# One order for all engines from the first pass on, in an attention and two feed-forward layers

## The chip, the cores and the metric

The kernel runs on one core of one Trainium2 chip. The metric is device time in microseconds (us) of one execution. Engines are called as the profile calls them: PE is TensorE's matmul queue and PEld its weight loads, DVE is VectorE, ACT is ScalarE, POOL is GpSimd, SP is SyncE, which issues the DMAs.

## What is computed

12480 tokens of 128 numbers go through an attention over 32 learned rows and then through two feed-forward layers of width 2048:

```python
h   = mab(I, x)                    # the 32 rows attend to all tokens
x1  = mab(x, h)                    # all tokens attend to the 32 results
a   = x1 @ w_in;  g = a * clip(a + 3, 0, 6) / 6
x2  = g @ w_out                    # first layer, 128 -> 2048 -> 128
r   = max(x2 @ w2_in, 0);  out = (r * r) @ w2_out   # second layer
# mab(q, kv): softmax(q @ kv.T / sqrt(128)) @ kv
```

The weights arrive as 64-bit floats.

## The kernel before

**Tiles and stages.** A first part, up to about 37 us, forms `h` from all tokens. Then the tokens run in 25 chunks of 512 (the last two 384 and 320), each in eight steps, so that a step `k` is a chunk `k // 8` and a pair of 128-wide slices `k % 8` of the 2048. The steps are numbered through, 0 to 199. A loop (L740) holds for each step `k`: `up1(k)` on PE (L575, two matmuls into a PSUM tile `h`), `gate1(k)` (ACT L588, then DVE L589), `high1` and `low1`, which split the gated tile into a rounded upper part and the rest, and `down1(k-2)`, which adds the step's share to `yacc`. The second layer follows eleven steps behind with `up2`, `relu2`, `square2`, `high2`, `low2` and `down2(k-14)`. At the end of a chunk `yacc` becomes `yh` (ACT L645) and `yl` (DVE L646).

**Two forms of a down matmul.** With both operands split, `down` (L621) issues six short matmuls in the fp32r form (L628). For the first steps, `k < N1` in the first layer and `k < N2` in the second, `down_whole` (L612) takes the unsplit tile and the unsplit weights in two fp32 matmuls (L616, each two records in the trace). A step in that form has no `high` and no `low`. N1 is 12 and N2 is 4.

**Weights.** Each of the four matrices comes in four pieces `a0` to `d3` (a: first up, b: first down, c: second up, d: second down). A conversion has a first stage (DVE L180 and L184, ACT L189), a second (DVE L191 and L195) and a third, an addition on POOL (L200). A cut then makes an upper part on ACT (L211) and a lower on DVE (L214). The `a` pieces are multiplied with the attention's result, `mix` (PE L455), `mix_high` (ACT L461) and `mix_low` (DVE L465), into the four quarters of `m4`, which `up1` reads.

**PSUM.** One pool of three buffers (`hp`, tag `h`) holds in turn the attention's scores `ps`, the products `mixed`, the turned weights `pt` and the tiles of `up1` and `up2`.

**What sets the order.** Up to `first.close()` (L733), and from step `KM` = 24 on, each engine runs its instructions in the order in which the program writes them. Between, a scheduler chooses the order of PE, DVE, ACT and POOL; only SP keeps the written order throughout. `PLAN` gives each weight piece the tick at which its conversion and its cut are handed to the scheduler, two ticks a step. From step 24 on, POOL first runs a one-column copy `turn` (L791) that reads the last tile DVE wrote in the step, and then `high1(k)`, so that POOL starts when DVE has come to that place.

Of the kernel before, what the change touches and what calls it, by code (L numbers as in the profile page):

```python
# [38 lines left out]

PLAN = {  # L40
    ("a", 0): (4, None),
    ("a", 1): (6, None),
    ("a", 2): (8, None),
    ("a", 3): (9, None),
    ("b", 0): (11, 51),
    ("b", 1): (16, 55),
    ("b", 2): (19, 42),
    ("b", 3): (23, 47),
    ("c", 0): (30, 33),
    ("c", 1): (35, 38),  # L50
    ("c", 2): (44, 47),
    ("c", 3): (50, 53),
    ("d", 0): (41, 59),
    ("d", 1): (47, 63),
    ("d", 2): (52, 55),
    ("d", 3): (55, 58),
}

CUTS = {"b": (2, 3, 0, 1), "c": (0, 1, 2, 3), "d": (2, 3, 0, 1)}

HIGH1_S = {13, 14, 18, 19, 20, 22, 23}
HIGH2_P = {6, 7, 10, 12}
N1, N2 = 12, 4
OFF = 11
L1, L2 = 2, 3
MIX = (0, 2, 4)
PRE = 22
KM = 24
# [7 lines left out]
def induced_attention_then_two_ffn(  # L76
# [93 lines left out]
    def lower_of(item):  # L170
        kind, q = item
        n = CUTS[kind].index(q)
        tag = f"w{kind}{CUTS[kind][n - 1]}" if n else {"b": "lb", "c": "lc", "d": "wc3"}[kind]
        return (wpool if kind == "b" else wpool2).tile([P, CW], F32R, tag=tag, name="wl")

    def convert(item):
        words = raws.pop(item)
# [12 lines left out]
        yield  # L190
        nc.vector.tensor_scalar(  # L191
            out=e, in0=e, scalar1=3, scalar2=0x3FFFFFFF,
            op0=ALU.logical_shift_left, op1=ALU.bitwise_and,
        )
        nc.vector.scalar_tensor_tensor(  # L195
            out=e, in0=high, scalar=0xC0000000, in1=e, op0=ALU.bitwise_and, op1=ALU.bitwise_or,
        )
        yield
# [7 lines left out]
    def cut(item):  # L206
        kind, q = item
        hi = (wpool if kind == "b" else wpool2).tile([P, CW], F32R, tag=f"h{kind}{q}", name="wh")
        w = whole.pop(item)
        assert ("a", q) not in whole or kind != "b"  # L210
        nc.scalar.copy(hi, w)  # L211
        yield
        lo = lower_of(item)
        nc.vector.tensor_tensor(out=lo, in0=w, in1=hi, op=ALU.subtract)  # L214
        parts[item] = hi, lo

# [5 lines left out]
    live, ticks = [], []  # L222

    def tick():
        n = len(ticks)
        ticks.append(n)
        for g in list(live):
            if next(g, live) is live:
                live.remove(g)
        for item, (when, cut_at) in PLAN.items():  # L230
            if when == n:
                load_until(item)
                live.append(convert(item))
                next(live[-1])
        for item, (when, cut_at) in PLAN.items():
            if cut_at == n:
                live.append(cut(item))
                next(live[-1])
# [16 lines left out]
    first = ExitStack()  # L255
    first.enter_context(tc.manual_schedule())
# [264 lines left out]
    def att_norm(c):  # L521
        a = att_weights(c)
        att[c] = a
        if c < TURNS:
# [3 lines left out]
            for u in range(2):  # L528
                last = nc.vector.tensor_tensor(
# [3 lines left out]
            return last  # L533
# [3 lines left out]
    def att_turn(c):  # L537
        a4 = att.pop(c)
        pt = hp.tile([P, CH], F32, tag="h", name="pt")
        to = pt.rearrange("p (b k t) -> p k b t", b=J, k=J)  # L540
# [6 lines left out]
        return nc.scalar.copy(a_t[c], pt)  # L547
# [45 lines left out]
    def high1(k):  # L593
# [3 lines left out]
        if k in HIGH1_S:  # L597
# [76 lines left out]
    def high2(k):  # L674
# [3 lines left out]
        if k in HIGH2_P or K - TAIL <= k < K - 1:  # L678
# [55 lines left out]
    behind = ExitStack()  # L734
    behind.enter_context(tc.issue_after(on_vector.ins))
    behind.enter_context(tc.issue_after(on_scalar.ins))
    for n in range(3):
        tick()
    assert len(ticks) == PRE, len(ticks)
    for k in range(K + OFF + L2 + 1):  # L740
        if k == KM:
            behind.close()
            ctx.enter_context(tc.manual_schedule())
# [3 lines left out]
        if k < KM:  # L747
            on(low1, k - 1)
        tick()
        on(gate1, k)  # L750
        if k < KM:
            on(high1, k)
# [13 lines left out]
        if k >= KM:  # L766
            on(down1, k - L1)
            on(down2, j - L2)
        behind_it = lo1[k - 1][:, 0, :1].bitcast(F32) if KM <= k < K else None
        if c + 1 < NCH:  # L770
            if p == 0 and LAST < c + 2 < NCH:
                load_x(c + 2)
            if p == 0:
                att_scores(c + 1)
                behind_it = att_shift(c + 1)
            if p == 1:
                att_exp(c + 1)
            if p == 2:
                behind_it = att_norm(c + 1)
            if p == 3:  # L780
                if c + 1 < TURNS:
                    att_turn(c + 1)
                else:
                    behind_it = att_spread(c + 1)
        if k < KM:
            on(down1, k - L1)
            on(down2, j - L2)
        elif k < K:

            n = behind_it.shape[0]  # L790
            nc.gpsimd.tensor_copy(turn[:n], behind_it)  # L791
            high1(k)
# [28 lines left out]
```

## Time and profile before

| | us |
|---|---|
| median of three runs (979.56 to 981.21) | 979.84 |
| profiled execution, its own time | 980.15 |
| its span in the trace | 978.4 |
| PE busy | 958.4 |
| DVE busy | 813.0 |
| ACT busy | 819.8 |
| POOL busy | 249.4 |

Busy time of PE counts modelled ends of matmuls that overlap, so the distance between starts of the same matmul in successive steps says more. A wait in brackets behind a row is the idle time of that engine just ahead of the instruction and what ended it. PEclk is the granted clock of TensorE as a share of full speed; its two levels are 2.4 GHz (1.00) and 1.2 GHz (0.50).

### The profile page before, as it was taken

What the parts mean: (1) busy time and instruction counts of PE and PEld (TensorE: products, weight loads), DVE (VectorE), ACT (ScalarE), POOL (GpSimd) and SP (SyncE); (2) the same over time, 40 slices, a digit from 0 to 9 for tenths busy, and PEclk for the clock granted to TensorE, in tenths of its full rate; (3) what the DMA queues carried; (4) which work ended last, traced back from release to release, by engine and by line L of the source; (5) the groups of instructions that cost most, each with busy time, mean ns of one, the idle gap of its engine ahead of it and who ended that gap; (6) DMA issues with size and microseconds to landing.
All of it is one profiled execution on the core that took longest, in us unless ns stands there. A gap on an engine that the chain in (4) does not pass through costs nothing.

```text
span 978.4 us, 12902 instructions
## 1 busy us (share of the span) xinstructions
PE 958.4 (98%) x4601; PEld 768.9 (79%) x4601; DVE 813.0 (83%) x999; ACT 819.8 (84%) x932; POOL 249.4 (25%) x390
## 2 busy tenths in 40 slices
PE   9789899999999999999999999999999999999998
PEld 7445588888888888888888888888888888888898
DVE  5889979888888888888888888888888888888774
ACT  6657798888888888888888888888888888888887
POOL 1222412222222222222222222222222222222222
PEclk9789999999999999999999999999999999999999
DMA  9610010010010110110110110110110100100000
GB/s 358 238 56 21 1 34 6 27 33 6 27 33 6 28 33 5 30 33 3 30 33 3 30 33 3 31 33 1 32 33 1 33 25 7 29 19 1 18 12 15
DMA packets 32111, 34.28 MB, mean 35 GB/s; under 512 B 7600, under 2 KB 24368, under 8 KB 31536
## 3 DMA queue, kind: packets, MB, share of 16 engines
q1 hardware_dynamic: 32048, 33.47, 11.0%
q8 instruction: 36, 0.59, 0.2%
q14 instruction: 27, 0.22, 0.1%
HBM read 21.18 MB, written 6.39 MB: 28 GB/s over the span
## 4 chain that ended last, share of the span: by engine, by line
PE 91%; DVE 5%; ACT 1%; POOL 1%; issue 1%; POOLq 0%; DVEq 0%
PE oacc L628 27%; PE h L657 26%; PE yacc L628 25%; PE h L580 9%; DVE g L589 1%; PE ps L478 1%; PE yacc L616 1%; POOL w L200 1%; PE xt L332 1%; DVE wl L214 1%; DVE lo L608 1%; PE s L312 1%; DVE cve L195 0%; DVE cve L184 0%; PE hacc L357 0%
## 5 line engine op out<-in xcount | busy, mean ns | idle before, releaser
L589 DVE SCALAR_TENSOR_TENSOR g<-g,h 128x1024 f32<-128x1024 f32 (+2 forms) x200 | 238.7, 1193 | 118.8 <-ACT g L588 115.2
L588 ACT ACTIVATE g<-h,three 128x1024 f32<-128x1024 f32 (+2 forms) x200 | 218.8, 1094 | 117.4 <-PE h L580 114.5
L692 DVE TENSOR_TENSOR lo<-g,hi 128x1024 fp32r<-128x1024 f32 (+3 forms) x197 | 235.0, 1193 | 9.7 <-PE oacc L628 6.0
L608 DVE TENSOR_TENSOR lo<-g,hi 128x1024 fp32r<-128x1024 f32 (+2 forms) x188 | 224.6, 1195 | 3.0 <-POOL hi L600 3.0
L672 ACT ACTIVATE g<-g 128x1024 f32<-128x1024 f32 (+3 forms) x201 | 206.0, 1025 | 0.4
L668 ACT ACTIVATE g<-h 128x1024 f32<-128x1024 f32 (+3 forms) x201 | 198.6, 989 | 4.8 <-PE h L657 3.6
L600 POOL TENSOR_SCALAR hi<-g 128x1024 fp32r<-128x1024 f32 (+2 forms) x181 | 187.4, 1035 | 22.9 <-DVE g L589 22.6
L684 ACT CAST hi<-g 128x1024 fp32r<-128x1024 f32 (+1 forms) x186 | 191.5, 1030 | 0.0
L657 PE MATMUL h<-yh,wh 128*128 128x512 f32 (+2 forms) x400 | 154.9, 387 | 3.8 <-DVE g L589 3.4
L657 PE MATMUL h<-yl,wh 128*128 128x512 f32 (+2 forms) x400 | 155.3, 388 | 0.0
L657 PE MATMUL h<-yh,wl 128*128 128x512 f32 (+2 forms) x400 | 154.9, 387 | 0.0
L580 PE MATMUL h<-at,m 128*128 128x512 f32 (+2 forms) x400 | 133.2, 414 | 3.6 <-ACT at L547 2.6
L628 PE MATMUL oacc<-hi,wh 128*128 128x512 f32 (+2 forms) x392 | 118.9, 384 | 0.0
L628 PE MATMUL oacc<-hi,wl 128*128 128x512 f32 (+2 forms) x392 | 118.9, 384 | 0.0
L628 PE MATMUL oacc<-lo,wh 128*128 128x512 f32 (+2 forms) x392 | 118.9, 384 | 0.0
L628 PE MATMUL yacc<-hi,wh 128*128 128x512 f32 (+2 forms) x376 | 114.4, 385 | 1.6 <-DVE yl L646 1.6
L628 PE MATMUL yacc<-hi,wl 128*128 128x512 f32 (+2 forms) x376 | 114.3, 385 | 0.0
L628 PE MATMUL yacc<-lo,wh 128*128 128x512 f32 (+2 forms) x376 | 113.7, 384 | 0.0
L791 POOL COPY turn<-lo 128x1 f32<-128x1 f32 x113 | 21.4, 189 | 343.4 <-DVE lo L608 343.4
L580 PEld LDWEIGHTS h<-at,m 128*128 128x128 f32 x400 | 74.3, 191 | 30.0 <-issue 9.5
L657 PEld LDWEIGHTS h<-yh,wh 128*128 128x128 f32 x400 | 75.1, 188 | 21.4 <-DVE g L589 4.2
L657 PEld LDWEIGHTS h<-yl,wh 128*128 128x128 f32 x400 | 75.2, 188 | 15.6 <-issue 0.2
(112 smaller groups left out, 926.0 us busy)
## 6 DMA issues: line engine op xcount, KB each, us to landing
outT<-osb SPq DMA_DIRECT2D x23, 256.0 KB, 2.2
xc<-in_xT SPq DMA_DIRECT2D x21, 256.0 KB, 2.8
xg<-in_xT SPq DMA_DIRECT2D x4, 1024.0 KB, 6.9
at<-ah SPq DMA_DIRECT2D x168, 16.0 KB, 1.8
at<-al SPq DMA_DIRECT2D x168, 16.0 KB, 1.8
raw<-in_w1a SPq DMA_DIRECT2D x4, 512.0 KB, 8.7
raw<-in_w1b SPq DMA_DIRECT2D x4, 512.0 KB, 7.5
raw<-in_w2a SPq DMA_DIRECT2D x4, 512.0 KB, 9.2
```

The costliest lines, as they stand in the source:

```text
L580: nc.tensor.matmul(h1[k][:, u, :size[c]], lhsT=m4[:, f * P:(f + 1) * P], rhs=a_t[c], start=True, stop=True)
L588: nc.scalar.activation(g1[k], h, AF.Relu, bias=three)
L589: nc.vector.scalar_tensor_tensor(out=g1[k], in0=g1[k], scalar=6.0, in1=h, op0=ALU.min, op1=ALU.mult)
L600: nc.gpsimd.tensor_scalar(out=hi1[k], in0=g1[k], scalar1=1.0, scalar2=1.0, op0=ALU.mult, op1=ALU.mult)
L608: nc.vector.tensor_tensor(out=lo1[k], in0=g1.pop(k), in1=hi1[k], op=ALU.subtract)
L628: nc.tensor.matmul(acc, lhsT=w[:, f * P:(f + 1) * P], rhs=g[:, u, :], start=(p == 0 and n == 0), stop=(p == NP - 1 and n == 5),)
L657: nc.tensor.matmul(h2[k][:, u, :size[c]], lhsT=w, rhs=y, start=(n == 0), stop=(n == 2))
L668: nc.scalar.activation(g2[k][:, u, :], h[:, u, :n], AF.Relu)
L672: nc.scalar.activation(g2[k][:, u, :], g2[k][:, u, :], AF.Square)
L684: nc.scalar.copy(hi2[k][:, u, :], g2[k][:, u, :])
L692: nc.vector.tensor_tensor(out=lo2[k][:, u, :], in0=g[:, u, :], in1=hi2[k][:, u, :], op=ALU.subtract)
L791: nc.gpsimd.tensor_copy(turn[:n], behind_it)
```

## The change

The order is now written out for all engines from the first pass to the end (`ctx.enter_context(tc.manual_schedule())` ahead of the first part). `PLAN`, `CUTS` and the two sets that chose an engine for the upper parts go. Tables say in which tick (`EARLY`) or step (`LATER`, `BESIDE`) a conversion's stages `1`, `2`, `3`, and the cuts `h` (upper) and `l` (lower), stand. What is named in `BESIDE` runs on POOL behind the one-column copy `turn`, now from before step 0: all third stages from `b1` on, and four of the lower parts (`b0`, `b1`, `c0`, `c1`). The other lower parts stay on DVE. `N1` goes from 12 to 16 and `N2` from 4 to 8. Of the `mix` products, two are now ahead of step 0 and the others in steps 2 and 3. The first chunk's scores are computed with the tokens in the partitions, so that its DVE transpose goes, and eight transposes of the identity (`fill`) stand on PE ahead of the first `pt`.

```diff
-    ("b", 0): (11, 51),
...
-    ("d", 3): (55, 58),
+LATER = {
+    0: "b3.1", 1: "b3.2", 3: "c0.1", 5: "c0.2 b0.h", 6: "c1.1 b1.h", 7: "c1.2 c0.h", 8: "b2.h",
...
+BESIDE = {
+    -1: "b1.3", 0: "b2.3", 1: "b3.3", 5: "c0.3", 6: "b0.l", 7: "c0.l", 8: "c1.3", 10: "c1.l",
...
-N1, N2 = 12, 4
+N1, N2 = 16, 8
...
-MIX = (0, 2, 4)
-PRE = 22
-KM = 24
+MIX = (2, 3)
...
+            if c == 0:
+                nc.tensor.matmul(ps[:, b, :], lhsT=tokens, rhs=ht4[:, 0, :], start=True, stop=True)
...
-        if k in HIGH1_S:
+        if k in BESIDE:
...
-        if k in HIGH2_P or K - TAIL <= k < K - 1:
+        if K - TAIL <= k < K - 1:
...
+    def beside(k, last):
+        names = BESIDE.get(k, "")
+        if names or (N1 <= k < K):
+            n = last.shape[0]
+            nc.gpsimd.tensor_copy(turn[:n], last)
+        jobs(names, nc.gpsimd)
+
     att_scores(0)
+    shift(("b", 1))
     att_shift(0)
     mix(0)
     att_exp(0)
     mix_high(0)
-    on_vector = att_norm(0)
+    mix(1)
+    mix_high(1)
+    fill(8, ap_, "o", 1)
+    att_norm(0)
+    att_turn(0)
     mix_low(0)
+    merge(("b", 1))
+    mix_low(1)
     tick()
-    on_scalar = att_turn(0)
-    tick()
-    first.close()
...
     for k in range(K + OFF + L2 + 1):
-        if k == KM:
-            behind.close()
-            ctx.enter_context(tc.manual_schedule())
...
+        last = jobs(LATER.get(k, "")) or last
...
+        beside(k, last)
+        on(high1, k)
```

First place: PE around step 0 (`ps` scores, `mixed` a mix product, `pt` the turned weights, `h` the tile of an `up1`, `yacc` a `down1`). Before:

```order
L478 MATMUL ps<-xlast,ht_75 32x128 x4
L455 MATMUL mixed<-wa,ht_75 128x512
L542 MATMUL pt<-ident_r,a_660 128x4x32 x4
L580 MATMUL h_699<-at,m_76 128x512 x2
L455 MATMUL mixed<-wa,ht_75 128x512
L478 MATMUL ps<-xlast,ht_75 32x128 x4
L580 MATMUL h_725<-at,m_76 128x512 x2
```

After:

```order
L496 MATMUL ps<-ht_75,xlast 128x32 x4
L470 MATMUL mixed<-wa,ht_75 128x512 x2
L248 MATMUL fill<-ident 128x128 x8
L567 MATMUL pt<-ident_r,a_671 128x128 x4
L605 MATMUL h_706<-at,m_76 128x512 x2
L605 MATMUL h_722<-at,m_76 128x512 x2
L605 MATMUL h_735<-at,m_76 128x512 x2
L470 MATMUL mixed<-wa,ht_75 128x512
```

The second mix product and the fill have moved ahead of `pt`, and three `up1` now follow each other where a mix product and scores stood between the first two.

Second place: DVE in steps 15 to 17 (`g` is the gate's second half, `lo` the lower part of a gated tile, `wl` that of a weight, `cve` a conversion stage, `st`, `nm`, `t` the scores of a later chunk). Before, from the gate of step 15 to that of step 17:

```order
L589 SCALAR_TENSOR_TENSOR g_1069<-g_1069,h_1055 128x1024
L191 TENSOR_SCALAR cve<-cve 128x512
L195 SCALAR_TENSOR_TENSOR cve<-raw,cve 128x512
L608 TENSOR_TENSOR lo_1099<-g_1069,hi_1072 128x1024
L214 TENSOR_TENSOR wl<-w_1101,wh 128x512
L692 TENSOR_TENSOR lo_1180<-g_1082,hi_1120 128x1024
L589 SCALAR_TENSOR_TENSOR g_1105<-g_1105,h_1096 128x1024
L487 STREAM_TRANSPOSE st<-ps 128x128
L214 TENSOR_TENSOR wl<-w_1182,wh 128x512
L490 TENSOR_REDUCE nm<-st 128x4
L214 TENSOR_TENSOR wl<-w_894,wh 128x512
L492 TENSOR_TENSOR t<-st,nm 128x128
```

After, from the gate of step 15 to that of step 17:

```order
L614 SCALAR_TENSOR_TENSOR g_1064<-g_1064,h_1061 128x1024
L190 TENSOR_SCALAR cve<-cve 128x512
L198 SCALAR_TENSOR_TENSOR cve<-raw,cve 128x512
L614 SCALAR_TENSOR_TENSOR g_1089<-g_1089,h_1086 128x1024
L226 TENSOR_TENSOR wl<-w_1059,wh 128x512
L175 TENSOR_SCALAR cve<-raw 128x512
L179 TENSOR_SCALAR cve<-cve 128x512
L509 STREAM_TRANSPOSE st<-ps 128x128
L512 TENSOR_REDUCE nm<-st 128x4
L514 TENSOR_TENSOR t<-st,nm 128x128
L614 SCALAR_TENSOR_TENSOR g_1134<-g_1134,h_1131 128x1024
```

Both `lo` and two of the three `wl` have gone from these steps.

Third place: POOL from the first `b` piece on (`w` a conversion's third stage). Before:

```order
L200 TENSOR_TENSOR w_532<-cve,cva 128x512
L200 TENSOR_TENSOR w_675<-cve,cva 128x512
L200 TENSOR_TENSOR w_695<-cve,cva 128x512
L200 TENSOR_TENSOR w_733<-cve,cva 128x512
L200 TENSOR_TENSOR w_802<-cve,cva 128x512
```

After:

```order
L210 TENSOR_TENSOR w_532<-cve,cva 128x512
L753 COPY turn<-cve 128x1
L210 TENSOR_TENSOR w_694<-cve,cva 128x512
L753 COPY turn<-cve 128x1
L210 TENSOR_TENSOR w_718<-cve,cva 128x512
L753 COPY turn<-cve 128x1
L210 TENSOR_TENSOR w_731<-cve,cva 128x512
L753 COPY turn<-cve 128x1
L210 TENSOR_TENSOR w_819<-cve,cva 128x512
L753 COPY turn<-cve 128x1
L226 TENSOR_TENSOR wl<-w_532,wh 128x512
```

Each addition now has a copy ahead of it that waits for DVE, and lower parts of weights stand on POOL.

## Rows read from the trace of the kernel before

**Rows 1.** Page: PE's busy time, and its granted clock in 40 slices.

```profile
PE 958.4 (98%) x4601; PEld 768.9 (79%) x4601; DVE 813.0 (83%) x999; ACT 819.8 (84%) x932; POOL 249.4 (25%) x390
...
PEclk9789999999999999999999999999999999999999
```

**Rows 2.** Windows: start and end, length, busy by engine, PEclk, DMA share, GB/s.

```profile
40.00:50.00 10.00, 7.17 (x21) 3.80 (x21) 9.71 (x21) 6.52 (x10) 2.80 (x3) 0.50 0.38 112
120.00:130.00 10.00, 10.00 (x45) 8.23 (x45) 8.89 (x13) 8.19 (x9) 0.76 (x1) 1.00 0.08 18
```

**Rows 3.** Waits of PE from 36 to 125 us: total us, times, longest.

```profile
PE h L657 <- DVE g L589: 3.4, 2, 2.1
PE h L580 <- ACT at L547: 2.6, 2, 1.9
...
PE yacc L616 <- POOL w L200: 1.7, 1, 1.7
PE yacc L628 <- DVE yl L646: 1.6, 1, 1.6
```

**Rows 4.** Timeline of PE: start us, us, line, out, in, records, wait.

```profile
37.62 1.62 PE L455 MATMUL mixed<-wa,ht 128*128 128x512 f32 x2
41.12 1.09 PE L542 MATMUL pt<-ident_r,a 128*128 128x128 f32 x4 [1.88 <-DVE a L529]
42.88 1.22 PE L580 MATMUL h<-at,m 128*128 128x512 f32 x2 [0.67 <-ACT at L547]
43.90 1.91 PE L455 MATMUL mixed<-wa,ht 128*128 128x512 f32 x2
...
73.37 1.03 PE L580 MATMUL h<-at,m 128*128 128x512 f32 x2
...
75.55 1.50 PE L580 MATMUL h<-at,m 128*128 128x512 f32 x4
...
90.79 1.02 PE L580 MATMUL h<-at,m 128*128 128x512 f32 x2
...
95.71 1.02 PE L580 MATMUL h<-at,m 128*128 128x512 f32 x2
...
126.43 0.62 PE L580 MATMUL h<-at,m 128*128 128x512 f32 x2
...
130.99 0.62 PE L580 MATMUL h<-at,m 128*128 128x512 f32 x2
```

**Rows 5.** Groups of instructions from 36 to 125 us: busy us, mean ns.

```profile
L589 DVE SCALAR_TENSOR_TENSOR g<-g,h 128x1024 f32<-128x1024 f32 x20 | 24.3, 1214 | 3.4 <-ACT g L588 3.3
L588 ACT ACTIVATE g<-h,three 128x1024 f32<-128x1024 f32 x20 | 22.3, 1113 | 8.3 <-PE h L580 6.3 <-PE yacc L616 1.8
...
L214 DVE TENSOR_TENSOR wl<-w,wh 128x512 fp32r<-128x512 f32 x12 | 13.0, 1092 | 1.8 <-ACT wh L211 1.8
L672 ACT ACTIVATE g<-g 128x1024 f32<-128x1024 f32 x9 | 9.5, 1059 | 0.1
...
L195 DVE SCALAR_TENSOR_TENSOR cve<-raw,cve 128x512 uint32<-128x512 uint32 x11 | 8.2, 746 | 0.0
...
L211 ACT CAST wh<-w 128x512 fp32r<-128x512 f32 x12 | 7.4, 614 | 4.2 <-POOL w L200 4.2
L189 ACT ACTIVATE cva<-raw 128x512 int32<-128x512 uint32 x10 | 6.6, 676 | 2.7 <-POOL w L200 2.7
...
L180 DVE TENSOR_SCALAR cve<-raw 128x512 uint32<-128x512 uint32 x10 | 4.2, 416 | 0.0
```

**Rows 6.** Timeline: a conversion's DVE work, and a gate, each beside POOL.

```profile
43.24 1.33 POOL L200 TENSOR_TENSOR w<-cve,cva 128x512 int32<-128x512 int32 x1 [10.44 <-DVE cve L195]
...
43.47 1.38 DVE L191 TENSOR_SCALAR cve<-cve 128x512 uint32<-128x512 uint32 x1
...
49.84 1.22 DVE L589 SCALAR_TENSOR_TENSOR g<-g,h 128x1024 f32<-128x1024 f32 x1
49.85 1.28 POOL L200 TENSOR_TENSOR w<-cve,cva 128x512 int32<-128x512 int32 x1 [2.60 <-ACT g L588]
```

More of the change, by code (lines that the diff above doesn't have):

```diff
@@ L194, in convert, with merge @@
         )
+    def merge(item):
+        high = raws.pop(item)[:, :, 1]
+        e, r = halves[item]
         nc.vector.scalar_tensor_tensor(
@@ L197, in convert, with second_stage, third_stage @@
         )
-        yield
+        return e[:, :1].bitcast(F32)
+    def second_stage(item):
+        shift(item)
+        return merge(item)
+    def third_stage(item):
+        e, r = halves.pop(item)
         w = float_of(item)
@@ L204, in convert, with upper, lower, jobs @@
             load_piece(waiting.pop(0))
-    def cut(item):
+    def upper(item):
         kind, q = item
         hi = (wpool if kind == "b" else wpool2).tile([P, CW], F32R, tag=f"h{kind}{q}", name="wh")
-        w = whole.pop(item)
         assert ("a", q) not in whole or kind != "b"
-        nc.scalar.copy(hi, w)
-        yield
+        nc.scalar.copy(hi, whole[item])
+        uppers[item] = hi
+    def lower(item, engine):
+        w, hi = whole[item], uppers.pop(item)
         lo = lower_of(item)
-        nc.vector.tensor_tensor(out=lo, in0=w, in1=hi, op=ALU.subtract)
+        engine.tensor_tensor(out=lo, in0=w, in1=hi, op=ALU.subtract)
         parts[item] = hi, lo
+        return lo[:, :1].bitcast(F32)
+    def jobs(names, engine=None):
+        last = None
+        for name in names.split():
+            item, what = (name[0], int(name[1])), name[3]
+            if what == "h":
+                upper(item)
+            elif what == "l":
+                last = lower(item, engine or nc.vector)
+            elif what == "3":
+                third_stage(item)
+            else:
+                last = (first_stage if what == "1" else second_stage)(item)
+        return last
     def fill(n, pool, tag, bufs):
@@ L220, in fill @@
             nc.tensor.transpose(t, ident, ident)
-    live, ticks = [], []
+    ticks = []
     def tick():
[L225 to L238, printed above, removed]
+        ticks.append(len(ticks))
+        return jobs(EARLY.get(ticks[-1], ""))
     todo = list(LOADS)
@@ L532, in att_norm @@
             att[c] = a4
-            return last
+            return a4[:, 0, 1, 1, :1].bitcast(F32)
         return a[:, 0, :1]
@@ L546, in att_turn @@
         a_t[c] = sp.tile([P, CH], F32R, tag="at", name="at")
-        return nc.scalar.copy(a_t[c], pt)
+        nc.scalar.copy(a_t[c], pt)
     def att_spread(c):
@@ L727, in induced_attention_then_two_ffn @@
     mix_high(0)
-    on_vector = att_norm(0)
+    mix(1)
[3 more added lines that the diff above has]
+    att_turn(0)
     mix_low(0)
+    merge(("b", 1))
+    mix_low(1)
     tick()
-    on_scalar = att_turn(0)
-    tick()
-    first.close()
[L734 to L739, printed above, removed]
+    beside(-1, tick())
+    assert len(ticks) == max(EARLY) + 1, len(ticks)
     for k in range(K + OFF + L2 + 1):
-        if k == KM:
-            behind.close()
-            ctx.enter_context(tc.manual_schedule())
         c, p = divmod(k, NP)
@@ L765, in induced_attention_then_two_ffn @@
             mix_low(q)
[L766 to L769, printed above, removed]
+        on(down1, k - L1)
+        on(down2, j - L2)
+        last = g1[k][:, 0, :1] if k < N1 else lo1[k - 1][:, 0, :1].bitcast(F32) if N1 < k < K else None
+        last = jobs(LATER.get(k, "")) or last
         if c + 1 < NCH:
@@ L772, in induced_attention_then_two_ffn @@
                 load_x(c + 2)
-            if p == 0:
+            stage = p - 2 if c == 0 else p
+            if stage == 0:
                 att_scores(c + 1)
-                behind_it = att_shift(c + 1)
-            if p == 1:
+                last = att_shift(c + 1)
+            if stage == 1:
                 att_exp(c + 1)
-            if p == 2:
-                behind_it = att_norm(c + 1)
-            if p == 3:
+            if stage == 2:
+                last = att_norm(c + 1)
+            if stage == 3:
                 if c + 1 < TURNS:
@@ L783, in induced_attention_then_two_ffn @@
                 else:
[L784 to L792, printed above, removed]
+                    last = att_spread(c + 1)
+        beside(k, last)
+        on(high1, k)
 _IN = ("x", "xT", "indT", "w1a", "w1b", "w2a", "w2b")
```

78 lines of the change are left out of this document (35 added, 43 removed), and 3 rows, old and new, of the table LATER.

## The prediction

> **What bounds the kernel now.** The page first: PE is busy 98% of the span, and its granted clock is at 9 in nearly all of the 40 slices, but at 7 and 8 in two of the first five [rows 1]. So the limit differs by stage, and I looked at the start in windows. From 120 us on PE is busy all the time at full clock; from 40 to 50 us it is busy 7.17 of 10 us at half clock, while DVE is busy 9.71 [rows 2]. The waits of PE up to 125 us say on whom it waited: on DVE's gate, on ACT's copy of the turned weights, on POOL's converted weights, on `yl` [rows 3]. Behind 125 us I found no such wait. The timeline of PE then gives the distances between the `up1` of successive steps, which is what a step costs [rows 4]. The reader is to see two regimes: a start in which DVE, ACT and POOL with the weight conversions hold PE up, and a long stretch in which PE alone counts. The change touches the first; what it can win is the time that PE loses there.
>
> **PE's own work in a step.** Steps that have only `up1` and the two-matmul `down1` take 75.55 - 73.37 = 2.18 us. A full step with all six-matmul groups takes 130.99 - 126.43 = 4.56, and a full step whose `down2` is unsplit takes 95.71 - 90.79 = 4.92 [rows 4]. A full split step is 20 equal matmuls, so one is 0.228 us, `up1` 0.46, a group of six 1.37, and an unsplit pair 2.18 - 0.46 = 1.72 to 1.73. So an unsplit pair costs PE 4.92 - 4.56 = 0.36 us more than the six; one mix product is half a pair, 0.87.
>
> **What PE loses now.** `up1` of step 0 starts at 42.88. That of step 21 is the row at 130.99 (I counted the `up1` pairs of the timeline), so step 22 starts at 130.99 + 4.56 = 135.5. Between are 92.7 us. PE's own work at full clock there: 22 `up1` 10.0; three mix products 2.6; `down1` of 0 to 19, twelve unsplit and eight split, 20.8 + 10.9; eleven `up2` 15.0; `down2` of 0 to 7, four and four, 6.9 + 5.5; attention's matmuls about 2 (an estimate; they are the same before and after but for the first scores). Together 73.7. So 19.0 us are lost to waits and to matmuls at half clock.
>
> **The change part by part.**
>
> *Unsplit steps.* Eight pairs of 0.36 more than before: +2.9 on PE, on the path. They take eight lower parts from DVE. Each has the elements of the gate, so about 1.2 us by the gate's mean of 1214 ns [rows 5], 9.6 in all, besides eight upper parts on ACT and POOL. All lie in steps 12 to 20, ahead of the waits of PE on the gate and on `yl` [rows 3].
>
> *Mix products.* One fewer behind step 0: -0.9 on PE there. It stands ahead of `pt` now. The first product started at 37.62 and its records last to 39.24; at half clock a product takes 1.84 (43.90 to the end at 45.81 less overlap) [rows 4]. So the second ends at 41.1, ACT's cast of it (as L211, 0.61 [rows 5]) at 41.7, and the cast for `pt`, which is behind it on ACT, at about 42.1. `pt` began at 41.12. I take +1.1 for the start of step 0. Bounds: if the clock stays full, the product ends at 40.2 and the gone transpose lets `pt` start about 0.6 earlier than before; if the eight fill transposes also run late at half clock, +2. DVE's merge of `b1` and second `mix_low`, which stand there too, end before step 0's gate needs DVE.
>
> *Fixed order and POOL behind DVE.* Now a conversion's DVE step can meet POOL: with POOL in its addition, L191 took 1.38 us [rows 6] where the like L180 takes 0.42 [rows 5]. The gate, which reads PSUM, ran 1.22 beside a POOL addition of 1.28 [rows 6], no longer than its mean. With the copy `turn`, POOL starts when DVE goes on to the next gate, so the addition lies beside it, at no cost. POOL's end some 0.3 us behind the gate's can hold the next DVE conversion; ten such places would be 3 us of DVE at most, which I put into the range. Queued behind each waiting copy are POOL's addition and, from step 16, `high1`; the cast on ACT and `down1` wait for these, one to three steps later.
>
> *Lower parts on POOL.* Four of them leave DVE, where the group's mean is 1.09 us [rows 5]: -4.4 on DVE in steps 6 to 13. By the Trainium skill, "GPSIMD Engine Reference", section 3.1, an elementwise addition costs GpSimd about twice what it costs VectorE, which speaks against such a move; by it DVE would save only some 0.65 each, 2.6 in all, and the total would not move, since POOL is far from being the bound.
>
> *What PE still waits for.* In written order each engine goes step by step, so I take each step at the longest of PE, DVE and ACT. By [rows 5]: gate 1.21 on DVE and 1.11 on ACT, conversion 0.83 and 1.16 on DVE and 0.68 on ACT, cast 0.61, `relu2` and `square2` 1.06 each. The normalization is taken as PE's wait of 1.88 [rows 4], an exponential as 0.3 (estimate: half a cast). Steps 0 to 13 come to: DVE 2.05, DVE 2.4, PE 3.4, PE 3.05, DVE 3.1, PE 2.8, ACT 2.4, DVE 2.4, PE 2.5, ACT 3.3, PE 2.2, PE 3.55, ACT 3.9, ACT 4.5, in all 41.55. PE's own part of them is 34.3. So PE waits 7.25. From step 14 on PE needs 4.9 to 5.9 a step and is the longest, except in step 17, where ACT has 5.8 against 5.3: 0.5. Waits 7.7. Behind step 22 the last lower parts (`d1` to `d3`) come in steps 22 to 26 on a DVE that has some 3.6 of 4.56 filled; I take nothing, and 0.6 if step 26 is not covered.
>
> **The sum.** Start 42.9 + 1.1; PE's work 73.7 + 2.9 - 0.9 = 75.7; waits 7.7: step 22 at 127.4 instead of 135.5, so 8.1 less. The profiled execution took 980.15, its span 978.4 and 1.75 around it, which stays; it lies 0.3 above the median of 979.84. 980.15 - 8.1 = **972.0 us**.
>
> **The rivals.**
>
> *PE never waits.* Three PSUM buffers let the steps overlap, so that the sum of the longest is too high: 972.0 - 7.7 = 964.3. For it: DVE's total over steps 0 to 13 is little above PE's. Against: the gate of each step needs its own ACT pass, and order is strict.
>
> *Waits stay at steps 16 to 19.* There DVE has attention, a lower part of a weight, a conversion and the first split tiles in each step, 3.6 to 5.0 us, and a POOL end on top. If PE waits 2.1 on a gate and 1.6 on `yl` as before [rows 3], 975.7; with a drop of the clock behind them, 977.
>
> *Slower: the clock stays low.* PE has gaps in steps 0 to 10 in my tally, and at half clock an unsplit pair takes 3.45 us, more than any engine's part of the step. Steps 2 to 13 are 33.4 us of PE work at full clock. Half clock over all of it adds 33.4, less the 7 of waits that it fills. It eats the gain from about 8.1 + 7 = 15 us of such work on; with two thirds (22 us) the time is 972.0 + 22 - 7 = 987. For it: the half clock from 40 to 50 us [rows 2] and the product of 1.91 [rows 4] in just this stage. Against: the steps from 73 us on ran at full clock with waits between, and PE is busy in 34.3 of 41.55 us here. The Trainium skill, "TensorE: Matmul & The Clock Gate", Part 1, has the low clock as the resting state, which sustained work ends and idle time brings back; by that rule the fill would help, and gaps as short as mine would not bring it back.
>
> **How the numbers follow.** Forecast, 968.5 to 975.5: 0.62. PE hardly waits, below 968.5: 0.13. Waits stay at 16 to 19, 975.5 to 978: 0.13. No change within 0.2% (about what a measurement of this kernel can tell; 2 us): 0.05, if half the conversions' steps collide with POOL. Slower: 0.07. The range of 8 in 10 reaches from 965.5, most of the floor with an early start, to 977.0, the second rival's end, which is also where 3 us of POOL ends and 2 of a late start would lead. Faster 0.88, same 0.05, slower 0.07.
>
> **What would show it.** `up1` of step 0 near 44 and of step 22 near 127; the counterpart of DVE's L191 back near L180's 0.42 and that of L214 well under 1.09; POOL's additions starting within the gates; no wait of PE over 1 us behind step 14; full clock from about step 2. I am wrong if a single weight piece is late for its fixed place: then DVE stands still with every gate behind it.

## The result and the profile after

The changed kernel takes 968.64 us (median of four runs, 967.99 to 969.93) against 979.7 for the kernel before beside it, a ratio of 0.9889 with a 95% interval of 0.9869 to 0.9908. So it is faster by about 11 us; the forecast was 8.1. The profiled execution took 967.99 us, its span is 966.2.

The page of after, PE's busy time and its granted clock in 40 slices:

```profile
PE 952.6 (99%) x4593; PEld 764.6 (79%) x4593; DVE 797.2 (83%) x986; ACT 814.6 (84%) x927; POOL 248.9 (26%) x412
...
PEclk9999999999999999999999999999999999999999
```

The 7 and the 8 in the early slices [rows 1] are gone. The same two windows as in [rows 2]:

```profile
40.00:50.00 10.00, 7.69 (x27) 3.99 (x25) 8.45 (x17) 6.58 (x10) 2.82 (x4) 0.92 0.41 111
120.00:130.00 10.00, 9.85 (x36) 6.81 (x37) 7.17 (x8) 7.74 (x9) 2.49 (x5) 1.00 0.18 50
```

From 40 to 50 us PE is about as busy as before, but at a granted clock of 0.92 instead of 0.50, and DVE has fallen from 9.71 to 8.45 us. The waits of PE from 36 to 125 us (total, times, longest), to be read against [rows 3]:

```profile
PE h L605 <- DVE g L614: 1.7, 1, 1.7
PE mixed L470 <- DVE g L614: 1.6, 1, 1.6
PE yacc L641 <- DVE yl L671: 1.3, 1, 1.3
...
PE h L605 <- ACT at L572: 0.7, 1, 0.7
PE oacc L641 <- POOL w L210: 0.5, 1, 0.5
```

The waits of the second layer's `h` on the gate (3.4) and of `yacc` on POOL (1.7) are gone. The timeline of PE (start, length, line, out and in, records, wait), the counterpart of [rows 4]:

```profile
37.28 1.10 PE L496 MATMUL ps<-ht,xlast 128*128 128x32 f32 x8 [0.70 <-DVE ht L449]
38.19 3.66 PE L470 MATMUL mixed<-wa,ht 128*128 128x512 f32 x4
41.68 1.04 PE L248 MATMUL fill<-ident 128*128 128x128 f32 x8
42.72 0.66 PE L567 MATMUL pt<-ident_r,a 128*128 128x128 f32 x4
44.06 1.66 PE L605 MATMUL h<-at,m 128*128 128x512 f32 x6 [0.68 <-ACT at L572]
...
126.49 1.03 PE L605 MATMUL h<-at,m 128*128 128x512 f32 x2
127.35 0.40 PE L682 MATMUL h<-yh,wh 128*128 128x512 f32 x1
```

`up1` of step 0 is at 44.06 (42.88 before) and that of step 22 at 126.49, 9.05 us earlier than the 135.54 of before. But the profiled execution is 980.15 - 967.99 = 12.16 us shorter. So 3.1 us more came from behind step 22, where PE waits in neither kernel. The steady step tells from where. Before, one step of many, in rows of PE (`up1`, the first `up2`, the first matmuls of `yacc` and `oacc`, the next `up1`):

```profile
607.69 0.62 PE L580 MATMUL h<-at,m 128*128 128x512 f32 x2
608.15 0.39 PE L657 MATMUL h<-yh,wh 128*128 128x512 f32 x1
...
609.53 0.62 PE L628 MATMUL yacc<-hi,wh 128*128 128x512 f32 x2
...
610.89 0.62 PE L628 MATMUL oacc<-hi,wh 128*128 128x512 f32 x2
...
612.25 0.62 PE L580 MATMUL h<-at,m 128*128 128x512 f32 x2
```

The same in after:

```profile
606.03 0.62 PE L605 MATMUL h<-at,m 128*128 128x512 f32 x2
606.49 0.39 PE L682 MATMUL h<-yh,wh 128*128 128x512 f32 x1
...
607.85 0.61 PE L653 MATMUL yacc<-hi,wh 128*128 128x512 f32 x2
...
609.21 0.61 PE L653 MATMUL oacc<-hi,wh 128*128 128x512 f32 x2
...
610.57 0.61 PE L605 MATMUL h<-at,m 128*128 128x512 f32 x2
```

612.25 - 607.69 = 4.56 against 610.57 - 606.03 = 4.54. The means over 90 steps, taken from the trace's times in ns (the steps of 15 chunks without the two that hold scores or follow them), are 4.553 and 4.533: the six `up2` take 1.375 us before and 1.360 after, the pair of `up1` 0.458 and 0.453, and the groups of `yacc` and `oacc` 1.360 in both. That is 0.020 us a step and, over the 177 steps behind step 22, 3.5 us. (The expectations below have 4.535 for 4.533 and 1.377 for 1.375, and so 3.3 us.) Nothing in the instructions, their order or their waits differs in these steps.

### The profile page after: what moved, and what is told of

It is laid out like the page before. It is cut to its first block, busy times and chain, and to the rows that moved or that the text cites. A ratio compares the mean times of both kernels' runs of the same rounds, so it can differ in the third digit from the quotient of the medians.

```text
span 966.2 us, 12901 instructions
## 1 busy us (share of the span) xinstructions
PE 952.6 (99%) x4593; PEld 764.6 (79%) x4593; DVE 797.2 (83%) x986; ACT 814.6 (84%) x927; POOL 248.9 (26%) x412
## 4 chain that ended last, share of the span: by engine, by line
PE 95%; DVE 4%; ACT 1%; issue 0%; POOL 0%; DVEq 0%; POOLq 0%
PE h L682 27%; PE oacc L653 26%; PE yacc L653 25%; PE h L605 9%; PE yacc L641 2%; PE oacc L641 1%; DVE g L614 1%; PE ps L498 1%; PE xt L347 1%; PE s L327 1%; PE mixed L470 0%; ACT g L613 0%; PE hacc L372 0%; PE fill L248 0%; DVE cve L179 0%
## 5 line engine op out<-in xcount | busy, mean ns | idle before, releaser
L717 DVE TENSOR_TENSOR lo<-g,hi 128x1024 fp32r<-128x1024 f32 (+3 forms) x193 | 229.4, 1189 | 7.8 <-PE oacc L653 4.1
L633 DVE TENSOR_TENSOR lo<-g,hi 128x1024 fp32r<-128x1024 f32 (+2 forms) x184 | 219.4, 1192 | 0.8 <-POOL hi L625 0.8
L605 PE MATMUL h<-at,m 128*128 128x512 f32 (+2 forms) x400 | 130.2, 407 | 2.4 <-DVE g L614 1.7
L653 PE MATMUL oacc<-hi,wh 128*128 128x512 f32 (+2 forms) x384 | 116.5, 384 | 0.0
L653 PE MATMUL oacc<-hi,wl 128*128 128x512 f32 (+2 forms) x384 | 116.4, 384 | 0.0
L653 PE MATMUL oacc<-lo,wh 128*128 128x512 f32 (+2 forms) x384 | 116.4, 384 | 0.0
L653 PE MATMUL yacc<-hi,wl 128*128 128x512 f32 (+2 forms) x368 | 111.2, 383 | 0.0
L653 PE MATMUL yacc<-lo,wh 128*128 128x512 f32 (+2 forms) x368 | 111.2, 383 | 0.0
L653 PE MATMUL yacc<-hi,wh 128*128 128x512 f32 (+2 forms) x368 | 111.1, 383 | 0.0
```

The costliest lines, as they stand in the source:

```text
L605: nc.tensor.matmul(h1[k][:, u, :size[c]], lhsT=m4[:, f * P:(f + 1) * P], rhs=a_t[c], start=True, stop=True)
L633: nc.vector.tensor_tensor(out=lo1[k], in0=g1.pop(k), in1=hi1[k], op=ALU.subtract)
L653: nc.tensor.matmul(acc, lhsT=w[:, f * P:(f + 1) * P], rhs=g[:, u, :], start=(p == 0 and n == 0), stop=(p == NP - 1 and n == 5),)
L717: nc.vector.tensor_tensor(out=lo2[k][:, u, :], in0=g[:, u, :], in1=hi2[k][:, u, :], op=ALU.subtract)
```

## The experiments

The table gathers what the traces say. "Step 0" and "step 22" are the starts of these `up1` in the profiled execution, "rest" is its own time less the start of step 22. The ratio is against the kernel before, run beside each. Step 0 differs by up to 3 us between executions of nearly the same code, and the runs of one kernel by 0.8 to 3.4, so for single terms the columns serve better than the medians.

| kernel | median us | ratio, 95% | step 0 | step 22 | rest | steady step |
|---|---|---|---|---|---|---|
| before | 979.84 | | 42.88 | 135.54 | 844.61 | 4.553 |
| before again | 979.74 | 0.9994 to 1.0012 | 42.72 | 135.37 | 844.62 | 4.553 |
| before, steps unsplit | 976.57 | 0.9956 to 0.9981 | 42.11 | 130.00 | 845.02 | 4.553 |
| before, banks exchanged | 979.65 | 0.9996 to 1.0015 | 42.43 | 134.87 | 844.61 | 4.553 |
| before, `at` placed as after | 975.79 | 0.9955 to 0.9980 | 42.73 | 133.66 | 841.05 | 4.533 |
| after | 968.64 | 0.9869 to 0.9908 | 44.06 | 126.49 | 841.50 | 4.533 |
| after again | 969.11 | 0.9886 to 0.9913 | 43.39 | 127.59 | 841.52 | 4.533 |
| after, split from step 12 | 968.01 | 0.9875 to 0.9902 | 42.53 | 127.79 | 841.49 | 4.533 |
| after, banks as before | 968.34 | 0.9875 to 0.9909 | 43.51 | 127.58 | 841.49 | 4.533 |
| after, old first scores | 971.35 | 0.9910 to 0.9939 | 42.08 | 125.53 | 845.02 | 4.553 |
| after, `at` placed as before | 971.56 | 0.9914 to 0.9941 | 43.41 | 127.75 | 845.02 | 4.553 |
| after, no copy ahead of POOL | 967.54 | 0.9870 to 0.9900 | 44.99 | 126.41 | 841.51 | 4.533 |
| after, lower parts on DVE | 970.13 | 0.9901 to 0.9928 | 45.02 | 129.03 | 841.50 | 4.533 |
| three edits together | 967.25 | 0.9873 to 0.9900 | 42.19 | 126.88 | 841.53 | 4.533 |

**Both kernels again, and each half of the change alone.** First question: is the pace of 4.533 an effect of the change or of one execution, and how much is owed to the unsplit steps, how much to the fixed order? The kernel after, unchanged:

> The changed kernel as it is. In the two profiled executions step 22 starts 9.0 us earlier than before, but the span is 12.2 us shorter, since the split steps behind it took 4.53 to 4.54 us instead of 4.55 to 4.56. Theory A (the pace is a matter of the execution): run again beside the kernel before, the difference is 9 us or so, and the pace of a step differs from run to run by 0.02. Theory B (the change altered the pace): 4.53 again, the kernel before at 4.55 again, and a difference of 11 to 12 us.

The kernel before, unchanged:

> The kernel before as it is, profiled again. Theory A: a step takes between 4.53 and 4.56 here, whichever the execution gives. Theory B: 4.55 to 4.56. Either way step 22 starts within 1 us of 135.5.

The kernel before with only the unsplit steps and the cuts that they need:

```diff
-    ("b", 0): (11, 51),
-    ("b", 1): (16, 55),
-    ("b", 2): (19, 42),
-    ("b", 3): (23, 47),
+    ("b", 0): (11, 42),
+    ("b", 1): (16, 47),
+    ("b", 2): (19, 51),
+    ("b", 3): (23, 55),
...
-CUTS = {"b": (2, 3, 0, 1), "c": (0, 1, 2, 3), "d": (2, 3, 0, 1)}
-N1, N2 = 12, 4
+CUTS = {"b": (0, 1, 2, 3), "c": (0, 1, 2, 3), "d": (0, 1, 2, 3)}
+N1, N2 = 16, 8
```

(the cuts of `d` follow in the same way)

> The kernel before with only the unsplit steps of the change (16 in the first layer, 8 in the second; the weights are cut in the order 0 to 3, and the cuts that an unsplit step would need later are put behind it). The scheduler still orders the first 24 steps. Theory A (two causes): the waits at steps 17 and 18, 2.1 and 1.6 us, and the half clock between go, about 5 to 6 us with the longer step, less 2.9 for eight dearer pairs on PE: 2 to 4 us faster than before. Theory B (unsplit steps are the gain): 8 us or more. Theory C (the fixed order is all the gain): 0 to 3 us slower.

The kernel after with `N1` back at 12, and so `b2` and `b3` cut first:

```diff
-    0: "b3.1", 1: "b3.2", 3: "c0.1", 5: "c0.2 b0.h", 6: "c1.1 b1.h", 7: "c1.2 c0.h", 8: "b2.h",
+    0: "b3.1", 1: "b3.2", 3: "c0.1", 5: "c0.2 b2.h", 6: "c1.1 b3.h", 7: "c1.2 c0.h", 8: "b0.h",
...
-N1, N2 = 16, 8
+N1, N2 = 12, 8
```

> The changed kernel with the first layer split from step 12 on again (the first down weights cut in the order 2, 3, 0, 1, each at the step where another of them stood, two of them a step earlier). Theory A (DVE and ACT needed the relief): PE gains 4 x 0.36 = 1.4 us, but ACT gets 1.05 us more in each of steps 12 to 15, 3.9 to 5.5 against 3.6 to 4.9 on PE, and DVE 1.2 in each of steps 13 to 16: 1 to 3 us slower than the changed kernel. Theory B (in fixed order the relief is not needed, since DVE is busy only 4.0 of 10 us from 90 to 100): 1 to 1.5 us faster than the changed kernel.

Measured: the pace belongs to the change (4.553 in three executions of the old program, 4.533 in three of the new). Unsplitting alone, under the scheduler, is worth 2.9 us in the medians: of the two waits of `up2` on the gate [rows 3], the 2.1 in step 17 goes and the 1.2 in step 13 stays, and the 1.6 on `yl` in step 18 goes too. In the fixed order the first layer's four unsplit steps are worth nothing that can be measured: split again from step 12, the kernel has 968.01 (967.56 to 969.28), and PE's waits between 36 and 130 us are still on `yl`, on the gate and on POOL, none of them on a split tile. So the order, with what it puts on POOL, is what removes the waits; the unsplit pairs are one way to get a part of that without it. Of the 11 us some 3.5 are the pace and 2.9 what unsplitting gave alone, so by difference between 4 and 5 us come only with the fixed order. How much of them the order itself gives, and how much the earlier `mix` product and the fill, is not shown: no run has the new order with the old split steps in both layers, and none leaves the fill out.

**Banks or addresses.** The tiles of the two programs lie in different places. `fill` takes the PSUM tag `o` first, so `yacc` and `oacc` exchange their banks; and since the first chunk has no `st`, the attention's small tiles are set aside in another order in SBUF, which moves `at`, the moving operand of `up1`, from byte 138720 of a partition to 138080; some weight tiles move too. Five kernels part this, each with the instructions of the steady steps unchanged. After with the banks of before:

```diff
-    fill(8, ap_, "o", 1)
+    fill(8, ap_, "y", 1)
```

> The kernel after with one edit: the eight fill transposes take the PSUM tag y instead of o. That gives the accumulators yacc and oacc back the PSUM banks that they have before (yacc 6, oacc 7; after has them the other way about); every instruction and every SBUF address stays as in after. Theory bank (the faster steady step of 4.535 us instead of 4.553 comes from the exchange of the two banks): the step goes back to about 4.553 and the time rises by about 3.3 us, to some 972. Theory SBUF (it comes from the other places of the weight tiles and of at in SBUF): the step stays at 4.535 and the time within 1 us of after, 968 to 970. Both: the first up1 stays at 43.4 to 44.1 us.

Before with the banks of after:

```diff
+    fill(1, ap_, "o", 1)
     on_vector = att_norm(0)
```

> The kernel before with one transpose of the identity into the tag o ahead of the first normalization: its accumulators' banks are exchanged as in after (yacc 7, oacc 6), its SBUF addresses stay those of before. Theory bank: the steady step falls from 4.553 to 4.535 us, the time by about 3.3 us to some 976.3, with the start as before (step 22 near 135.5 us). Theory SBUF: the step stays at 4.553, the time at 979 to 980.

After with the first scores as in before (scores, transpose and the layout of `pt`):

```diff
-        ps = hp.tile([P, J, M] if c == 0 else [M * nb, n], F32, tag="h", name="ps")
+        ps = hp.tile([M * nb, n], F32, tag="h", name="ps")
...
-        st = att.pop(c)
-        if c:
-            ps = st
-            st = sp.tile([M * nb, n // M, M], F32, tag="st", name="st", bufs=1)
-            nc.vector.transpose(st.rearrange("p b i -> p (b i)"), ps)
+        st = sp.tile([M * nb, n // M, M], F32, tag="st", name="st", bufs=1)
+        nc.vector.transpose(st.rearrange("p b i -> p (b i)"), att.pop(c))
```

> The kernel after with the first chunk's scores as before (tokens as the moving operand, DVE transpose, the old layout of the turned weights), the rest as in after. The at and st tiles lie again where they are before (at at 138720 instead of 138080); the accumulators' banks and the weight tiles stay as in after. Theory SBUF with at as the cause: the steady step goes back to 4.553. Theory bank: it stays at 4.535. For the start: the transposed scores took PE 1.10 us instead of 0.43 and the gone DVE transpose saved about the same, so I expect the first up1 between 0.5 us earlier and 0.7 later than in after, and the time within 1 us of after where the bank theory holds.

The banks do nothing: the rest is 841.49 with the banks of before in after, 844.61 with those of after in before. My first theory fell there. The old scores brought the slow pace back, and with it `at` had moved. Step 0 starts at 42.08 with them, 2.0 us earlier than in after and outside what I had expected, and step 22 at 125.53, 1 us earlier than in after and 2 earlier than in after again. So the new form of the first scores seems to cost time at the start. That is the row of 1.10 us for `ps` above, where before had 0.43:

```profile
37.27 0.43 PE L478 MATMUL ps<-xlast,ht 128*32 128x128 f32 x8 [0.70 <-DVE ht L434]
```

From the start of `ps` to DVE's reduction, which now needs no transpose, it is 1.20 us in after (37.28 to 38.48) and 0.90 in the kernel with the old scores (36.93 to 37.83). That is 0.3 us in DVE's chain. Of the rest of the 2 us at step 0, 0.35 stands already at the start of `ps`, and the other 1.3 goes with the clock, which was at half in after for most of the two products and at full in this kernel; so what the form itself costs is not shown beyond the 0.3. Two more kernels move `at` and no instruction. After, with `st` set aside for the first chunk too, unused:

```diff
+        if c == 0:
+            sp.tile([P, J, M], F32, tag="st", name="st", bufs=1)
```

> The kernel after with one tile more: for the first chunk, too, the buffer st is set aside ahead of the attention's other tiles, and nothing writes it. No instruction changes; the attention's small tiles move up in SBUF by 640 bytes in each partition, and of what PE reads only at, the moving operand of up1, moves (from 138080 to 138720, where it is before). Theory placement (the place of at sets the pace of up1 and of the up2 behind it): six up2 take 1.377 us instead of 1.360, the steady step 4.553 instead of 4.535, the time some 3.3 us more than after, 971.5 to 973. Rival (the slower step of old_scores came from its scores' form or its DVE transpose, not from the place): the step stays at 4.535 and the time at 968 to 970.

Before, with the other small tiles set aside ahead of `st`:

```diff
+    for tag, shape, dt, n in (
+        ("nm", [P, J], F32, 2), ("t", [P, J, M], F32, 2), ("e", [P, J, M], F32, 2),
...
+        ("a", [P, J, M], F32, 2), ("a4", [P, J, 2, 2, M], F32R, 1), ("at", [P, CH], F32R, 2),
+    ):
+        sp.tile(shape, dt, tag=tag, name=tag, bufs=n)
     att_scores(0)
```

> The kernel before with the attention's small tiles set aside in the order that they have in after, so that at lies at 138080 and st behind it; no instruction changes, the accumulators' banks and the weight tiles stay as before. Theory placement: the steady step falls from 4.553 to 4.535 us and the time by about 3.3 us, to some 976.2, with the start as before (step 22 near 135.5 us). Rival: the step stays at 4.553, the time at 979 to 980.

A steady step of after with `at` at 138720:

```profile
604.86 0.62 PE L607 MATMUL h<-at,m 128*128 128x512 f32 x2
605.32 0.39 PE L684 MATMUL h<-yh,wh 128*128 128x512 f32 x1
...
606.70 0.62 PE L655 MATMUL yacc<-hi,wh 128*128 128x512 f32 x2
...
609.42 0.62 PE L607 MATMUL h<-at,m 128*128 128x512 f32 x2
```

And of before with `at` at 138080:

```profile
603.68 0.61 PE L580 MATMUL h<-at,m 128*128 128x512 f32 x2
604.14 0.39 PE L657 MATMUL h<-yh,wh 128*128 128x512 f32 x1
...
605.50 0.62 PE L628 MATMUL yacc<-hi,wh 128*128 128x512 f32 x2
...
608.22 0.62 PE L580 MATMUL h<-at,m 128*128 128x512 f32 x2
```

From `up2` to `yacc` it is 1.38 in the first and 1.36 in the second, from `up1` to `up1` 4.56 and 4.54. The rest is 845.02 against 841.50, and 841.05 against 844.61: the 640 bytes are worth 3.5 us in either program. What moves is the whole set of the attention's small tiles; `at` is the only one that PE reads in a steady step, and the others are in use only in the steps that hold attention. That `at` is the tile is therefore argued, that it is the placement is shown. One thing more speaks for `at`: in the slow place the distances between starts leave their 227 ns with the first matmul that reads it. From the first `up1` to the fourth `up2` the starts are 234, 224, 232, 233 and 231 ns apart (means over 90 steps), and for the rest of the step 227 again.

**The copy ahead of POOL.** After without it up to step 15:

```diff
             n = last.shape[0]
-            nc.gpsimd.tensor_copy(turn[:n], last)
+            if k >= N1:
+                nc.gpsimd.tensor_copy(turn[:n], last)
```

> The kernel after without the one-column copy ahead of POOL's conversions of steps -1 to 15, so that POOL starts an addition or a lower part as soon as its operands are there (from step 16 on the copy stays). Theory A (of the recorded sum: POOL beside DVE's conversion stages costs DVE up to a microsecond each time, and the copy keeps that off): some second stages on DVE take 1.2 to 1.4 us again instead of 0.46, step 22 starts 1 to 4 us later, the time rises by as much. Rival: POOL's work starts in nearly the same places, or earlier and so with less waiting for converted weights; time within 1 us of after, or up to 1.5 below.

DVE does run into POOL, but in first stages (L175, L179) and not in the second stages that I named. DVE and POOL of this kernel around 64 us (records merged where they follow each other):

```profile
64.40 0.74 DVE L175 TENSOR_SCALAR cve<-raw 128x512 uint32<-128x512 uint32 x1
64.80 2.90 POOL L226 TENSOR_TENSOR wl<-w,wh 128x512 fp32r<-128x512 f32 x2
65.17 1.39 DVE L179 TENSOR_SCALAR cve<-cve 128x512 f32<-128x512 f32 x1
```

In the group by lines from 36 to 115 us L179 rises from a mean of 427 ns to 719. That is 2.9 us over ten instructions, all of it in three of them, and none reaches PE: step 22 is at 126.41 against 126.49, the median 967.54. The copy saves DVE time that is not the bound. Theory A of the expectation fell in its price, the rival held.

**The lower parts on DVE.** After with `b0`, `b1`, `c0` and `c1` cut on DVE in the same steps:

```diff
-    0: "b3.1", 1: "b3.2", 3: "c0.1", 5: "c0.2 b0.h", 6: "c1.1 b1.h", 7: "c1.2 c0.h", 8: "b2.h",
-    9: "c2.1 b3.h", 10: "c1.h", 11: "c2.2", 12: "d0.1 d0.2", 13: "c3.1 c2.h c2.l",
+    0: "b3.1", 1: "b3.2", 3: "c0.1", 5: "c0.2 b0.h", 6: "c1.1 b1.h b0.l", 7: "c1.2 c0.h c0.l", 8: "b2.h",
+    9: "c2.1 b3.h", 10: "c1.h c1.l", 11: "c2.2", 12: "d0.1 d0.2", 13: "c3.1 c2.h c2.l b1.l",
```

(and out of `BESIDE`)

> The kernel after with the four lower parts b0, b1, c0, c1 back on DVE, in the steps in which POOL has them. By the recorded working DVE gets 0.69 us (the mean of L226 in after) in steps 6, 7, 10 and 13, of which only those count where DVE was already the longest: 0 to 2 us, so 969 to 971. Rival: DVE is late for the next gate each time and every step behind it is moved, as in before: 2.8 us and more, 971.5 or above. Steady step 4.535 in either case.

It takes 970.13 us, within the 969 to 971 that I expected, 1.5 more than after. Its start is by chance that of the kernel without the copy (45.02 and 44.99), so these two compare best: step 22 is 2.6 us later. The four instructions would be 2.8 us if all were on the path, but that is not how it comes. PE of this kernel, and its windows:

```profile
73.54 3.00 PE L641 MATMUL yacc<-g,w 128*128 128x512 f32 x4 [1.88 <-DVE yl L671]
75.55 1.84 PE L605 MATMUL h<-at,m 128*128 128x512 f32 x2
```

```profile
70.00:74.00 4.00, 2.12 (x6) 0.72 (x5) 3.90 (x8) 3.40 (x7) 1.41 (x2) 1.00 0.00 0
74.00:78.00 4.00, 4.00 (x9) 2.21 (x8) 2.84 (x7) 0.94 (x2) 0.00 (x0) 0.57 0.00 0
```

The wait on `yl` has grown from 1.3 to 1.88, and behind it the granted clock falls to 0.57: the next pair of `up1` takes 1.84 instead of 1.03. Half a microsecond of waiting more costs another 1.7 in the clock (an estimate: 4 us at 0.57 instead of 1.00). It is the mechanism of the recorded third rival, in small.

**Three edits together.** Split from step 12, no copy up to step 11, the old first scores with `at` kept at 138080:

> The kernel after with what was a little faster alone, together: N1 = 12 with the cuts of b in the order 2, 3, 0, 1 (968.0 alone), no copy ahead of POOL's conversions up to step 11 (967.5 alone), and the first scores in the form of before (whose first up1 came at 42.1 us and step 22 at 125.5, while its steady step was 4.553), with the attention's tiles set aside so that at stays at 138080. If the three gains at the start add and placement holds: step 22 of the first layer at about 124 us, steady step 4.535, time 965.5 to 967. If they are the same few tenths of the clock's rise at the start and of a wait that moves: 967.5 to 969, no faster than split_from_12.

967.25 (966.78 to 968.41) can't be told from the others. Step 0 is at 42.19, but the third mix product then waits 3.1 us for a gate, and from 48 to 52 us the granted clock is 0.50. Step 22 is at 126.88 and not near 124, so the gains do not add. No version that I ran beats the changed kernel by more than can be measured.

## Why the prediction was right

The time lies in the range and in the forecast's own case. The gain was put 3 us too small, and the reason is one term that the sum did not have, the pace behind step 22. The start itself came out near the forecast, in part by luck.

**What bounds, and where.** Right. The gain that I worked out lies ahead of step 22 (9.05 us in the two profiled executions and 7.8 in the two others, against 8.1), and PE waits nowhere behind it.

**PE's own work, unsplit pairs.** Right in the size of a pair: a step of after with an unsplit `down2` has 4.91, as I read from before:

```profile
106.04 1.03 PE L605 MATMUL h<-at,m 128*128 128x512 f32 x2
...
110.95 1.03 PE L605 MATMUL h<-at,m 128*128 128x512 f32 x2
```

The last of the eight dear pairs reaches into step 22 (0.86 from its `up1` to `up2` instead of 0.46), which is the 0.4 between 841.05 and 841.50. Wrong in the term that I took as fixed: 4.56 for a full step [rows 4] was carried over to the kernel after, and 0.020 less over the 177 steps behind step 22 are 3.5 us, as much as the change of place measured by itself.

**The start.** 44.0 forecast, 44.06 in the profiled execution. The chain is the one that I put, the second product, ACT's cast of it, and behind that the cast for `pt`:

```profile
41.88 0.59 ACT L476 CAST m<-mixed 128x512 fp32r<-128x512 f32 x1 [0.96 <-PE mixed L470]
42.37 0.30 ACT L549 CAST a<-a 128x128 fp32r<-128x128 f32 x1
```

But two errors cancel, and the near hit is luck to that extent. The products end at 41.85 and not at 41.1, most of it because the new scores take PE 1.10 instead of 0.43; and `pt` takes 0.66, where I carried over the 1.09 of before. I also counted, in the lower bound, on 0.6 from the gone transpose; with the new scores DVE's reduction comes 0.3 later, not earlier. And the number depends on the clock: the two products take 3.66 us where it was at half for most of them, and 1.96 where it stays at full, as in the kernel split from step 12. In the kernels with the new scores step 0 lay between 42.5 and 45.0, about the two ends of the bounds that I gave.

**POOL behind DVE.** Mostly as put. The groups from 36 to 125 us in after, to be read against [rows 5]:

```profile
L614 DVE SCALAR_TENSOR_TENSOR g<-g,h 128x1024 f32<-128x1024 f32 x22 | 26.8, 1220 | 13.2 <-ACT g L613 13.2
...
L210 POOL TENSOR_TENSOR w<-cve,cva 128x512 int32<-128x512 int32 x11 | 14.1, 1281 | 0.3 <-issue 0.3
...
L198 DVE SCALAR_TENSOR_TENSOR cve<-raw,cve 128x512 uint32<-128x512 uint32 x11 | 7.6, 693 | 0.4
...
L226 POOL TENSOR_TENSOR wl<-w,wh 128x512 fp32r<-128x512 f32 x4 | 5.1, 1281 | 0.0
L190 DVE TENSOR_SCALAR cve<-cve 128x512 uint32<-128x512 uint32 x11 | 5.0, 455 | 0.2 <-issue 0.2
...
L226 DVE TENSOR_TENSOR wl<-w,wh 128x512 fp32r<-128x512 f32 x5 | 3.4, 687 | 2.0 <-ACT wh L220 2.0
```

L190, the counterpart of L191, has 455 ns (0.79 us once, beside a lower part on POOL, and 0.42 to 0.43 else), and DVE's lower parts 687 ns instead of 1092. DVE and POOL in the timeline of after:

```profile
48.27 1.27 POOL L210 TENSOR_TENSOR w<-cve,cva 128x512 int32<-128x512 int32 x1
...
48.78 1.22 DVE L614 SCALAR_TENSOR_TENSOR g<-g,h 128x1024 f32<-128x1024 f32 x1 [0.78 <-ACT g L613]
...
63.88 1.28 POOL L210 TENSOR_TENSOR w<-cve,cva 128x512 int32<-128x512 int32 x1 [0.28 <-issue]
64.33 1.11 DVE L175 TENSOR_SCALAR cve<-raw 128x512 uint32<-128x512 uint32 x1
```

All but two of the additions start up to 0.7 us ahead of a gate or within one, as [rows 6] had them, and the gate keeps its 1.22; the two, at 90.31 and 94.44, ran beside no work of DVE. Where POOL's end reaches into the next conversion, L175 takes 1.11 instead of 0.42, as I put it into the range; with the 0.79 of L190 that is two places, not ten. The Trainium skill, "SBUF — State Buffer", section "Who interferes with whom", says that such a one-input operation can run in VectorE's two-port mode, and that it and a GpSimd operation then shut each other out for a whole instruction. The collisions shown here, 1.11 in this timeline and 1.39 without the copy, agree with it as far as POOL's rough spans tell.

**Lower parts on POOL.** 1281 ns on POOL against 687 on DVE is a ratio of 1.86. The "about twice" that the prediction had from the Trainium skill ("GPSIMD Engine Reference", section 3.1) agrees with it. My -4.4 for DVE should have been -2.7: the 1092 of [rows 5] is a mean of seven cuts at 0.68 to 0.69 us and five at 1.5 to 1.8, and each of the five ran beside POOL. I held that this difference would not move the total, which no run tests; moving the four cuts back to DVE costs 1.5 to 2.6 us, some 1.7 of it by the clock.

**The waits that are left.** 7.7 forecast; the waits behind step 0 in the list above come to 1.7 + 1.6 + 1.3 + 0.5 = 5.1. From step 0 to step 22 I had 83.4 us and the profiled execution has 82.43, the one again 84.2. The single steps are less well hit than their sum: step 4 was put at 3.1 and took 2.19, step 9 3.3 and 1.88, step 10 2.2 and 3.71. The rule that each step takes the longest of its engines is thus not how the waits came. PE started `up1` of steps 0 to 2 within 1.1 us, in the three PSUM buffers, and then stood twice until a gate had freed one; those are the waits of 1.6 and 1.7.

**The rivals.** PE still waits, so the floor is out. The waits at steps 16 to 19 are gone: behind step 14 the longest is 0.5. The clock did not stay low, but it did fall once or twice somewhere between 37 and 56 us in all these kernels: in after during the mix products; in the same kernel run again there and from 52 to 56 us (0.57); where it is split from step 12, from 52 to 56 us alone (0.60). Where it falls behind step 0, the way from step 0 to step 22 takes 84.1 to 84.3 us with the same instructions (after again, banks as before, `at` placed as before), and 82.4 in after, where it fell ahead of it; so an early step 0 can be lost again. One reading of mine was wrong: I set against the low clock that the steps of before from 73 us on ran at full clock with waits between. Behind the wait in step 17 they did not, as the timeline and the window from 110 to 112 us show:

```profile
109.30 0.50 PE L657 MATMUL h<-yh,wh 128*128 128x512 f32 x1 [2.12 <-DVE g L589]
```

```profile
110.00:112.00 2.00, 2.00 (x6) 1.55 (x5) 2.00 (x5) 0.19 (x2) 0.38 (x1) 0.50 0.00 0
```

I had held, with the Trainium skill's "TensorE: Matmul & The Clock Gate", Part 1, that gaps as short as these would not bring the low level back. The clock fell behind this wait of 2.12 us, and behind one of 1.88 in the kernel with the lower parts on DVE; there the measurement decides.

## What to carry to other kernels

Compare the steady step of two programs to a hundredth of a microsecond before you credit a difference to the part that was edited: over 177 steps, 0.020 us made 3.5 of these 11 us, and it came from where tiles happen to lie. In a start that is short of work for PE, a delay can cost several times its length: here 0.6 us more of waiting brought the granted clock down behind it, for another 1.7; so count such delays by what follows them. And a copy or a move that spares a busy engine is worth something only where that engine ends the wait.

## What the runs showed that I had not expected

**Matmuls depend on where the attention's tiles lie, most likely the moving operand.** With `at` at byte 138720 of a partition eight matmuls, two `up1` and the six `up2` behind them, take 1.833 us in a steady step; at 138080 they take 1.813. The `up2` read other tiles, at the same addresses in both, and the first three of them are slowed all the same; the last three and the twelve matmuls behind them are not. Even at 138080 the six `up2` take 1.385 in one step of each chunk, the second, which starts behind the fp32 matmuls of the scores, and 1.360 in the other seven. At 138720 they take 1.375 in these seven, and in the second step 1.387, where the group of `yacc` takes 1.381 too. What the mechanism is stays open: two placements were tried, no third.

**The clock's fall moves by microseconds.** With the new first scores the start of step 0 spread from 42.53 us, where the granted clock was 1.00 from 36 to 44 us, to 45.02, where it was 0.60 and 0.54 in the two halves of that stretch. Single runs of one kernel lay 1 to 3 us apart, while the rest behind step 22 repeated to 0.04 us within each program and placement.
